# Output stores, two evacuations and the loads of batch 1 in a fused linear-attention and GELU-MLP kernel

## The chip, the core and the metric

The kernel runs on one core of a Trainium2 chip. The metric is the device time of one execution in microseconds (us). Before the change the median of 15 runs is 319.3 us, with runs from 317.35 to 322.01. The engines are called PE (matrix products; PEld is its weight load), DVE (vector), ACT (scalar), POOL (GpSimd) and SP (sync, which here only issues DMAs). An engine's queue is the list of instructions that it executes in order; a DMA is issued by an instruction in one of these queues and then runs by itself.

## The reference

The inputs q, k and v have 8 batches, 8 heads, 576 positions and 64 features, all float32. The attention has no softmax: q and k go through a ReLU, and each is multiplied by a cosine and by a sine of its position.

```
phi(x) = concat(relu(x) * cos(pi/2 * pos/576), relu(x) * sin(pi/2 * pos/576))
kv  = sum over positions of phi(k)^T v          # 128 x 64 per head
z   = sum over positions of phi(k)
x   = (phi(q) kv) / (phi(q) . z + 1e-6)         # 4608 tokens x 512
h   = x w_in                                    # 512 -> 2048
out = (h * sigmoid(1.702 h)) w_out              # 2048 -> 512
```

## The kernel before

**Attention, by batch.** For a batch, three float32 tiles qf, vf and kf are loaded. A main load (load_part, L79) brings positions 0 to 511 and a tail load (load_tail, L84) positions 512 to 575; a main is 1024 KB in rows of 1 KB, a tail 128 KB in rows of 256 bytes. These tiles have two buffers each. Then follow prep_q (L219: ReLU of q into qn, bf16), the transposition of qn (on PE for batches 0 and 1, L234; by DMA on SP for the others, L246), the product with cos and sin (qT, L244 or L256, on DVE), prep_v (L265: v times cos and times sin into vt), prep_k (L258: ReLU of k into kr), unit_kv (L280: 40 small matmuls, then casts zbuf and kvs on DVE), unit_den (L305: 32 matmuls, then the reciprocal on DVE), unit_spread (L330: matmuls, then four copies invb on ACT) and unit_num (L346: 16 matmuls, then four DVE multiplications at L359 by the inverse, "the division", which write xT). unit_spread and unit_num run for two halves of the positions.

**MLP, by block.** The 4608 tokens are cut into 9 blocks of 512 tokens. A block runs 16 tiles of mm1 (L373: four matmuls into a PSUM tile hps, GELU on ACT into g) and then mm2 for four chunks t of 128 tokens (L395: 16 matmuls into a PSUM tile, in four parts of four). After a chunk's last part, the PSUM tile is copied into an SBUF tile ysb (the evacuation, L404 to L408), and one or two DMAs (pieces, L379) store it on SP's queue (L410). ysb comes from ypool with three buffers (L162). hps and yps have two PSUM buffers each. In block 0 the four chunks are computed in turn, part by part (t = n % 4), with chunks 0 and 1 in hps and 2 and 3 in yps; chunks 1 and 3 are copied by DVE (L406), all others by ACT (L408). In the later blocks one chunk follows the other, and ACT copies all. The last chunk of the last block is mm2_last (L412), with its stores on SP and ACT.

**Order.** The order on every engine is the order in which the program emits the instructions. The loop of L483 lays it out by hand in steps n = 0 to 31 of one block: step n emits a tile of mm1 (n < 16) or a part of mm2, and then the attention pieces of the next batch that are listed in work[n]. Steps n = 32 to 39 (L531) hold only such pieces. In block 0, for batch 1, prep_q is at n = 6, prep_v from 8 to 12, prep_k at 13 and 14, unit_kv at 15, unit_den at 18, unit_spread at 22 and 28, unit_num at 25 and 31. So in block 0 the second unit_num stands behind the last part of mm2 and its evacuation, and block 1 begins with mm1, which reads xT of batch 1. In later blocks everything of the next batch starts at n = 0, and the second unit_num is at n = 28, with three parts of mm2 behind it.

**Loads.** Batch 0 is loaded by SP, its tails by ACT. POOL then issues the four pieces of w_in (L454), after a small copy of one element of vf that makes it wait for that load (L452). SP waits for w_in's second piece (L455, a DMA of one element) and issues the mains of batch 1 in the order q, v, k (L457). POOL waits for w_in's third piece (L458), issues the three tails of batch 1 (L459), waits for batch 1's vf (L460) and issues the four pieces of w_out (L462). SP waits for w_out's third piece (L463) and loads batch 2. From batch 3 on, load_all(b + 1) stands behind the DMA transposes of batch b on SP.

Of the kernel before, what the change touches and what calls it, by code (L numbers as in the profile page):

```python
# [12 lines left out]
F32 = mybir.dt.float32  # L13
# [15 lines left out]
def kernel(  # L29
# [9 lines left out]
    nc = tc.nc  # L39
    B, H, S, D = q.shape  # L40
    d_model = H * D
# [21 lines left out]
    def hps_tile():  # L63
        return ps.tile([128, TB], F32, name="hps", bufs=2)

    def yps_tile():
        return ps.tile([128, TB], F32, name="yps", bufs=2)
# [9 lines left out]
    state = {b: {} for b in range(B)}  # L77

    def load_part(t, src, b, h0, h1):  # L79
        nc.sync.dma_start(  # L80
            out=t[:, 256 * h0:256 * h1].rearrange("p (h e) -> p h e", h=h1 - h0),
            in_=src[b, h0:h1, 0:512, :].rearrange("h (p c) d -> p h (c d)", c=4))

    def load_tail(t, src, b, on):  # L84
        on.dma_start(
            out=t[0:64, 2048:2560].rearrange("p (h d) -> p h d", h=H),
            in_=src[b, :, 512:576, :].rearrange("h p d -> p h d"))

    SRC = (("qf", q), ("vf", v), ("kf", k))

    def load_new(b):
        for name, _ in SRC:
            state[b][name] = two.tile([128, 2560], F32, name=name)

    def load_tails(b, on):
        for name, src in SRC:
            load_tail(state[b][name], src, b, on)

    def load_mains(b):
        for name, src in SRC:  # L100
            load_part(state[b][name], src, b, 0, H)
# [57 lines left out]
    tmp.close()  # L159

    gpool = ctx.enter_context(tc.tile_pool(name="gpool", bufs=18))
    ypool = ctx.enter_context(tc.tile_pool(name="ypool", bufs=3))  # L162

    kr = one.tile([128, 5, NP, 128], BF16, name="kr")
    vt = one.tile([128, 5, H, VW], BF16, name="vt")
# [35 lines left out]
    w_in_sb = one.tile([128, NP, d_ff], BF16)  # L201
# [171 lines left out]
    def mm1(i, fc):  # L373
        hps = hps_tile()
        for kc in range(NP):
            mm1_part(hps, i, fc, kc)
        gelu(hps, fc)

    def pieces(m):  # L379

        got, g = [], m * 128
        while g < m * 128 + 128:
            b, r = divmod(g, S)
            if r < 512:
                n = min(128 - r % 128, m * 128 + 128 - g)
                got.append((g - m * 128, n, b * S + 4 * (r % 128) + r // 128, 4))
            else:
                n = min(S - r, m * 128 + 128 - g)
                got.append((g - m * 128, n, b * S + r, 1))
            g += n  # L390
        return got

    cur = {}

    def mm2(i, t, part):  # L395

        if part == 0:
            cur[t] = hps_tile() if i == 0 and t < 2 else yps_tile()
        yps = cur[t]
        for fc in range(part * 4, part * 4 + 4):  # L400
            nc.tensor.matmul(yps, gT[fc][:, ds(t * 128, 128)], w_out_sb[:, fc, :],  # L401
                             start=(fc == 0), stop=(fc == FC - 1))
        if part == 3:
            ysb = ypool.tile([128, d_model], F32, name="ysb")  # L404
            if i == 0 and t % 2:
                nc.vector.tensor_copy(ysb, yps)  # L406
            else:
                nc.scalar.copy(ysb, yps)  # L408
            for (p0, n, row, step) in pieces(i * 4 + t):
                nc.sync.dma_start(out=out[row:row + (n - 1) * step + 1:step, :], in_=ysb[p0:p0 + n, :])  # L410

    def mm2_last(i, t):  # L412

        yps = yps_tile()
        ysb = ypool.tile([128, d_model], F32, name="ysb")
        hd = d_model // 2
        for n in range(2):
            cols = ds(n * hd, hd)
            if n == 1:
                yps = yps_tile()  # L420
            for fc in range(FC):
                nc.tensor.matmul(yps[:, 0:hd], gT[fc][:, ds(t * 128, 128)], w_out_sb[:, fc, cols],  # L422
                                 start=(fc == 0), stop=(fc == FC - 1))
            if n == 0:
                nc.scalar.copy(ysb[:, cols], yps[:, 0:hd])
            else:
                nc.vector.tensor_copy(ysb[:, cols], yps[:, 0:hd])  # L427
            for m, (p0, cnt, row, step) in enumerate(pieces(i * 4 + t)):
                (nc.sync if m == 0 else nc.scalar).dma_start(out=out[row:row + (cnt - 1) * step + 1:step, cols],
                                                             in_=ysb[p0:p0 + cnt, cols])  # L430


    junk = const.tile([1, 16], F32)
# [20 lines left out]
        nc.gpsimd.dma_start(out=w_in_sb[:, :, ts(g, 512)], in_=win_r[:, :, ts(g, 512)])  # L454
    nc.sync.dma_start(out=junk[:, 8:9], in_=w_in_sb[0:1, 0, 1022:1024].bitcast(F32))  # L455
    load_new(1)
    load_mains(1)  # L457
    nc.gpsimd.tensor_copy(junk[:, 2:3], w_in_sb[0:1, 0, 1534:1535])  # L458
    load_tails(1, nc.gpsimd)  # L459
    nc.gpsimd.tensor_copy(junk[:, 1:2], state[1]["vf"][0:1, 0:1])  # L460
    for g in range(4):
        nc.gpsimd.dma_start(out=w_out_sb[:, ts(g, 4), :], in_=wout_r[:, ts(g, 4), :])  # L462
# [20 lines left out]
    for i in range(NBLK):  # L483
        work = {n: [] for n in range(40)}
        b = i + 1

        def at(n, f, *a):
            work[n].append(lambda: f(*a))

        if b < B:  # L490
            k0 = 6 if i == 0 else 0
            at(k0, prep_new, b)
            at(k0, prep_q, b, 0)
            at(k0, prep_q, b, 1)
            if i == 0:
                for j in range(NP):
                    at(k0 + 2 + j, transpose_pe, b, j, 0)
                    at(k0 + 2 + j, transpose_pe, b, j, 1)
            else:
                at(k0, transpose_dma, b)  # L500
                if b + 1 < B:
                    at(k0 + 1, load_all, b + 1)
            for c in range(5):
                for cs in range(2):
                    at(k0 + 2 + c, prep_v, b, c, cs)
            at(k0 + 7, prep_k, b, 0, 4)
            at(k0 + 7, prep_k_tail, b)
            at(k0 + 8, prep_k, b, 4, 8)
            if i > 0:
                for j in range(NP):  # L510
                    at(k0 + 9 + j, prep_trig, b, j)
            k1 = 15 if i == 0 else 12
            at(k1, unit_kv, b)
            at(k1 + 3, unit_den, b)
            for hf in range(2):
                at(k1 + 7 + 6 * hf, unit_spread, b, hf)
                at(k1 + 10 + 6 * hf, unit_num, b, hf)
        for n in range(32):
            if n < FC:
                if i > 0 or n > 3:  # L520
                    mm1(i, n)
            elif i == 0:
                mm2(i, n % 4, (n - FC) // 4)
            elif i == NBLK - 1 and n >= 28:
                if n == 28:
                    mm2_last(i, 3)
            else:
                mm2(i, (n - FC) // 4, n % 4)
            for f in work[n]:
                f()  # L530
        for n in range(32, 40):  # L531
            for f in work[n]:
                f()


# [28 lines left out]
```

## Time and profile before

| what | us |
|---|---|
| median of 15 runs | 319.3 |
| the profiled execution: its time | 319.18 |
| its span, first to last instruction | 317.2 |
| PE busy | 301.1 |
| DVE busy | 135.4 |
| ACT busy | 135.5 |
| POOL busy | 18.6 |
| first mm1 of block 1 starts | 64.19 |
| first mm1 of block 2 starts | 98.36 |
| last evacuation (DVE, L427) ends | 313.49 |

All numbers of the prediction come from one profiled execution. A line of a timeline gives start, duration, engine, line, operation, tiles written and read, and in brackets how long the engine had been idle and what ended that. Several equal instructions in a row are one line with xN, whose duration is that of the whole group. Instructions that overlap in a pipeline have durations longer than the distance between their starts. In a table of stages, the number behind the busy times is the clock that PE was granted (1.00 is full speed), then the share of time in which the DMA engines were busy, and GB/s. "To landing" is the time from a DMA's issue to its completion. A DMA with a cast (w_in and w_out) is counted by the bytes that it writes, half of those that it reads.

### The profile page before, as it was taken

How to read it: one execution, taken by the hardware profiler on the slowest of the kernel's cores; microseconds unless marked ns; L12 is line 12 of the kernel's file. 1: busy time of each engine (PE TensorE's matmuls, PEld its weight loads, DVE VectorE, ACT ScalarE, POOL GpSimd, SP SyncE). 2: the span in 40 equal slices, each digit the busy share in tenths (PEclk: the TensorE clock that was granted, in tenths of full speed). 3: DMA queues.
4: the chain of work that ended last, by engine and by line, in shares of the span. 5: the costliest groups of instructions: out<-in, count | busy, mean ns of one | idle time of the engine just before them, and what ended most of it. 6: DMA issues, size and time to landing. Idle time of an engine off the chain costs nothing.

```text
span 317.2 us, 5510 instructions
## 1 busy us (share of the span) xinstructions
PE 301.1 (95%) x2178; PEld 140.4 (44%) x2216; DVE 135.4 (43%) x344; ACT 135.5 (43%) x260; POOL 18.6 (6%) x56
## 2 busy tenths in 40 slices
PE   8799979689999999999999999999999999999994
PEld 3344544234444544454445444444444444444443
DVE  4852864195319451954193618541854110000000
ACT  5544511336334634363436343634462446217511
POOL 7802400000000000000000000000000000000000
PEclk9999999979999999999999999999999999999999
DMA  7999999936923495349435953593330220011022
GB/s 209 267 205 293 243 187 294 274 74 199 286 67 85 108 354 111 100 132 331 96 83 141 336 97 98 158 320 82 83 60 0 69 66 0 35 66 33 2 66 66
DMA packets 60908, 45.83 MB, mean 144 GB/s; under 512 B 27380, under 2 KB 56308, under 8 KB 60884
## 3 DMA queue, kind: packets, MB, share of 16 engines
q1 hardware_dynamic: 54772, 40.38, 47.6%
q0 software_dynamic: 4368, 4.59, 8.9%
q10 hardware_dynamic: 1744, 0.52, 0.8%
q8 instruction: 17, 0.28, 0.4%
q14 instruction: 7, 0.06, 0.1%
HBM read 36.70 MB, written 9.44 MB: 145 GB/s over the span
## 4 chain that ended last, share of the span: by engine, by line
PE 82%; DMA 11%; DVE 3%; issue 1%; SPq 1%; POOL 0%; ACT 0%; DVEq 0%; ACTq 0%
PE yps L401 36%; PE hps L365 36%; DMA vf<-in_v_dram 7%; PE at L288 3%; PE at L356 3%; DMA w_in_sb<-in_moe_w_in_dram 2%; PE hps L401 2%; DMA out_dram<-ysb 2%; DVE vt L277 1%; PE at L314 1%; PE yps L422 1%; PE at L338 1%; DVE qT L244 1%; DVE kr L217 0%; POOL w_in_sb L454 0%
## 5 line engine op out<-in xcount | busy, mean ns | idle before, releaser
L365 PE MATMUL hps<-xT,w_in_sb 128*128 128x512 bf16 x551 | 127.6, 382 | 5.0 <-DVE xT L359 3.8
L401 PE MATMUL yps<-w_out_sb,g 128*128 128x512 bf16 x509 | 118.8, 380 | 0.9 <-issue 0.2
L370 ACT ACTIVATE g<-hps 128x512 bf16<-128x512 f32 x142 | 84.7, 597 | 58.3 <-PE hps L365 55.6
L365 PEld LDWEIGHTS <-w_in_sb 128*128 128x128 bf16 x576 | 55.7, 98 | 72.6 <-issue 9.0
L401 PEld LDWEIGHTS <-g 128*128 128x128 bf16 x560 | 51.9, 98 | 63.4 <-issue 2.9
L408 ACT COPY ysb<-yps 128x512 f32<-128x512 f32 x32 | 18.7, 585 | 83.4 <-PE yps L401 54.1
L359 DVE TENSOR_TENSOR xT<-at,invb 128x288 bf16<-128x288 f32 x64 | 24.7, 450 | 62.0 <-PE at L356 62.0
L343 ACT COPY invb<-at 128x288 f32<-128x288 f32 x60 | 19.7, 419 | 21.0 <-PE at L338 21.0
L256 DVE TENSOR_TENSOR qT<-qTr,trig 128x1152 bf16<-128x1152 bf16 x24 | 16.6, 754 | 22.4 <-DMA qTr<-qn 19.8
L427 DVE COPY ysb<-yps 128x256 f32<-128x256 f32 x1 | 0.4, 425 | 56.7 <-PE yps L422 56.7
L277 DVE TENSOR_SCALAR vt<-vf,cosw 128x512 bf16<-128x512 f32 (+1 forms) x40 | 19.2, 488 | 1.2 <-DMA vf<-in_v_dram 1.2
L217 DVE TENSOR_SCALAR qn<-qf 128x512 bf16<-128x512 f32 (+2 forms) x52 | 14.2, 342 | 8.5 <-DMA qf<-in_q_dram 8.5
L277 DVE TENSOR_SCALAR vt<-vf,sinw 128x512 bf16<-128x512 f32 (+1 forms) x36 | 17.6, 490 | 0.0
L75 PE MATMUL hps<-warm 128*128 128x512 bf16 x47 | 13.8, 455 | 1.2 <-DVE halfpi L121 1.2
L288 PE MATMUL at<-vt,kr 128*64 128x130 bf16 x320 | 10.9, 221 | 3.6 <-ACT kr L215 1.8
L356 PE MATMUL at<-qT,kvs 64*64 64x288 bf16 x256 | 12.2, 289 | 0.4 <-ACT invb L343 0.3
L288 PEld LDWEIGHTS <-kr 128*64 128x64 bf16 x320 | 9.3, 109 | 7.2 <-issue 2.5
L217 DVE TENSOR_SCALAR kr<-kf 128x1024 bf16<-128x1024 f32 (+1 forms) x23 | 12.3, 588 | 0.0
L356 PEld LDWEIGHTS <-kvs 64*64 64x64 bf16 x256 | 6.4, 105 | 8.0 <-issue 7.7
L75 PEld LDWEIGHTS <-warm 128*128 128x128 bf16 x47 | 5.0, 113 | 8.3 <-issue 3.9
L401 PE MATMUL hps<-w_out_sb,g 128*128 128x512 bf16 x30 | 7.6, 380 | 0.1
L323 DVE RECIPROCAL den<-den 128x144 f32<-128x144 f32 x7 | 7.4, 1053 | 0.2
(79 smaller groups left out, 98.3 us busy)
## 6 DMA issues: line engine op xcount, KB each, us to landing
qf<-in_q_dram SPq DMA_DIRECT2D x8, 1024.0 KB, 6.6
vf<-in_v_dram SPq DMA_DIRECT2D x8, 1024.0 KB, 9.4
kf<-in_k_dram SPq DMA_DIRECT2D x7, 1024.0 KB, 12.2
out_dram<-ysb SPq DMA_DIRECT2D x38, 128.0 KB, 2.4
out_dram<-ysb SPq DMA_DIRECT2D x16, 256.0 KB, 2.3
w_in_sb<-in_moe_w_in_dram POOLq DMA_DIRECT2D x4, 512.0 KB, 8.9
w_out_sb<-in_moe_w_out_dram POOLq DMA_DIRECT2D x4, 512.0 KB, 9.4
kf<-in_k_dram SPq DMA_DIRECT2D x2, 512.0 KB, 11.4
```

The lines of the kernel that those rows point to most:

```text
L75: nc.tensor.matmul(wps, warm[:, 0:128], warm, start=True, stop=True)
L217: on.tensor_scalar(o, i, 0.0, None, op0=MAX)
L256: nc.vector.tensor_tensor(s["qT"][:, j], s["qTr"][:, j].unsqueeze(1).to_broadcast([128, 2, S]), trig, op=MUL)
L277: on.tensor_scalar(o, i, w, None, op0=MUL)
L288: nc.tensor.matmul(kv4[j // 2][w:w + 64, j % 2], kr[:, c, j, 64 * hh:64 * hh + 64], vt[:, c, 2 * j + hh, :], start=(c == 0), stop=(c == 4))
L343: nc.scalar.copy(invb, bps[j][:, 0:HF])
L356: nc.tensor.matmul(num_ps[j][w:w + 64, 0:HF], s["kvs"][j][r:r + 64, cs, :], s["qT"][r:r + 64, j, cs, ds(hf * HF, HF)], start=(cs == 0), st ...
L359: nc.vector.tensor_tensor(xT[:, j, ds(b * S + hf * HF, HF)], t[:, 0:HF], s["invb"][j, hf], op=MUL)
L365: nc.tensor.matmul(hps, w_in_sb[:, kc, ds(fc * 128, 128)], xT[:, kc, ds(i * TB, TB)], start=(kc == 0), stop=(kc == NP - 1))
L370: nc.scalar.activation(g, hps, AF.Gelu_apprx_sigmoid)
L401: nc.tensor.matmul(yps, gT[fc][:, ds(t * 128, 128)], w_out_sb[:, fc, :], start=(fc == 0), stop=(fc == FC - 1))
L408: nc.scalar.copy(ysb, yps)
```

## The change

Four things are edited. ypool gets a fourth buffer. The evacuation becomes a function of its own, evac, whose stores are issued by POOL instead of SP; the stores of mm2_last stay where they were. In block 0 the chunks t = 0 and 1 are evacuated by ACT after their last part, and chunks 2 and 3 by DVE after the whole of block 0's work, that is behind the second unit_num of batch 1 and its division. The six loads of batch 1 are all issued by SP, in the order main of q, tail of q, main of v, tail of v, tail of k, main of k; POOL's wait for w_in's third piece goes.

```diff
-    ypool = ctx.enter_context(tc.tile_pool(name="ypool", bufs=3))
+    ypool = ctx.enter_context(tc.tile_pool(name="ypool", bufs=4))
...
-        if part == 3:
-            ysb = ypool.tile([128, d_model], F32, name="ysb")
-            if i == 0 and t % 2:
-                nc.vector.tensor_copy(ysb, yps)
-            else:
-                nc.scalar.copy(ysb, yps)
-            for (p0, n, row, step) in pieces(i * 4 + t):
-                nc.sync.dma_start(out=out[row:row + (n - 1) * step + 1:step, :], in_=ysb[p0:p0 + n, :])
+        if part == 3 and (i > 0 or t < 2):
+            evac(i, t)
+
+    def evac(i, t, on=None):
+        ysb = ypool.tile([128, d_model], F32, name="ysb")
+        if on is nc.vector:
+            nc.vector.tensor_copy(ysb, cur[t])
+        else:
+            nc.scalar.copy(ysb, cur[t])
+        for (p0, n, row, step) in pieces(i * 4 + t):
+            nc.gpsimd.dma_start(out=out[row:row + (n - 1) * step + 1:step, :], in_=ysb[p0:p0 + n, :])
...
-    load_mains(1)
-    nc.gpsimd.tensor_copy(junk[:, 2:3], w_in_sb[0:1, 0, 1534:1535])
-    load_tails(1, nc.gpsimd)
+    for name, src in SRC:
+        if name == "kf":
+            load_tail(state[1][name], src, 1, nc.sync)
+        load_part(state[1][name], src, 1, 0, H)
+        if name != "kf":
+            load_tail(state[1][name], src, 1, nc.sync)
     nc.gpsimd.tensor_copy(junk[:, 1:2], state[1]["vf"][0:1, 0:1])
...
         for n in range(32, 40):
             for f in work[n]:
                 f()
+        if i == 0:
+            for t in range(2, 4):
+                evac(i, t, nc.vector)
```

## The prediction

> **What bounds the kernel now.** I read the page first: engine shares, then the 40 slices, then the chain of work that ended last.
>
> ```profile
> span 317.2 us, 5510 instructions
> ...
> PE 301.1 (95%) x2178; PEld 140.4 (44%) x2216; DVE 135.4 (43%) x344; ACT 135.5 (43%) x260; POOL 18.6 (6%) x56
> ...
> PE   8799979689999999999999999999999999999994
> ```
>
> PE is busy 95% of the span, and after slice 8 (about 65 us) it is never below nine tenths until the end. So nothing on DVE, ACT, POOL or SP earns time in the later blocks unless it makes PE wait there. What can be won lies where PE has holes: before 65 us. The list of waits names two that the change touches. The larger is in the chain between 56 and 68 us (start, length, what):
>
> ```profile
> 57.84 5.12 DMA out_dram<-ysb
> ...
> 63.08 0.06 DVE ysb L406
> ...
> 63.69 0.46 DVE xT L359
> ...
> 64.19 2.96 PE hps L365 x7
> ```
>
> The DVE timeline says why:
>
> ```profile
> 58.13 0.69 DVE L406 COPY ysb<-hps 128x512 f32<-128x512 f32 x1 [2.53 <-PE hps L401]
> 63.08 0.69 DVE L406 COPY ysb<-yps 128x512 f32<-128x512 f32 x1 [4.26 <-DMA out_dram<-ysb]
> 63.69 1.54 DVE L359 TENSOR_TENSOR xT<-at,invb 128x288 bf16<-128x288 f32 x4
> ```
>
> The fourth evacuation of block 0 needs a fourth ysb; three exist, so DVE waits until the first store has landed (62.96). Behind it in DVE's order stand the four divisions (L359) that block 1's first matmuls read. PE ended unit_num of batch 1 at 60.43 and starts mm1 of block 1 at 64.19. The wait has an after-effect. Stages of 1 us, PE alone (busy, instructions, granted clock, DMA share, GB/s):
>
> ```profile
> 64.00:65.00 1.00, 0.81 (x3) 1.00 0.37 141
> 65.00:66.00 1.00, 1.00 (x3) 0.61 0.33 121
> 66.00:67.00 1.00, 1.00 (x3) 0.50 0.00 0
> 67.00:68.00 1.00, 0.78 (x3) 0.50 0.00 0
> 68.00:69.00 1.00, 1.00 (x4) 0.68 0.66 131
> 69.00:70.00 1.00, 1.00 (x7) 1.00 0.52 108
> ```
>
> After a hole of 3.76 us the granted clock falls to half for about 3.4 us. The second hole is in block 0:
>
> ```profile
> 35.01 0.49 DVE L277 TENSOR_SCALAR vt<-vf,cosw 128x512 bf16<-128x512 f32 x1 [1.23 <-DMA vf<-in_v_dram]
> ...
> 42.08 1.70 PE L288 MATMUL at<-vt,kr 128*64 128x130 bf16 x40 [1.63 <-DVE kr L217]
> ```
>
> DVE works without a gap from 35.01, when batch 1's vf lands, to the end of kr at 42.97; unit_kv waits for it and takes 1.70 us with a stop inside (its next runs take 1.32). So about 2.0 us of PE time hang on DVE's start, hence on vf's landing.
>
> **Part 1: evacuations of t=2 and t=3 behind the division, four buffers.** Either edit alone removes the wait on the store. DVE is then free from 55.6 on, since t=1 goes to ACT. ACT copies t=0 at 56.92, the four invb at 57.40 to 58.71, then t=1 until about 59.3, where it now copies t=2. Nothing of ACT's is due before the first gelu, and mm1 needs t=1's hps buffer only at its second tile. In blocks 1 and 2 the first division starts 0.54 us after unit_num's first matmul (88.90 to 89.44, 95.14 to 95.69). unit_num starts at 59.75, so the division starts at 60.29, lasts 0.45, and mm1 starts 0.05 later, at 60.79. Saved: 64.19 - 60.79 = **3.40 us**. What is late next is the division itself: kc=1 to 3 come at DVE's pace (0.36 us each, as before at 64.19, 64.55, 64.92, 65.28), which is in both kernels.
>
> The hole left is 0.36 us. The 1.63 us hole at 40.45 left the granted clock at 1.00 in every stage behind it, so I take the half-clock stretch as gone. Before, the starts from 65.28 to 68.65 are 8 intervals in 3.37 us; later blocks run 45 matmuls in 9.71 us, 0.216 each, so 8 take 1.73. Saved: **1.65 us** (0 if the clock falls all the same).
>
> The two copies come back on DVE behind the division: 2 x 0.61 us (start to start). DVE's preparation of batch 2 starts at 61.74 + 1.22 = 62.96, 2.17 us after mm1's start instead of 0.95, and mm1 itself now runs 1.65 us faster. The cover: unit_kv(2) falls at 77.80 - 3.40 - 1.65 = 72.75, kr is ready 7.4 us after 62.96, at 70.4. The thin place is unit_den(2): 81.79 - 5.05 = 76.74. It needs qT and zbuf. SP's transposes start 1.78 us after prep_q's start (66.92 against 65.14): 64.74; first qT 8.21 us later (75.13 against 66.92): 72.95; four qT 2.68 and four zbuf casts 0.74: 76.37. Slack 0.37 us, where it was 2.26. In blocks 2 and 3 the same stretch from transposes to qT took 8.77 and 8.66 us, 0.5 longer, and prep_q may be stretched (part 2). I charge **0.2 us**, bounds 0 and 0.9.
>
> **Part 2: stores on POOL's queue.** 52 issues leave SP (0.48 us median) for POOL, which is idle after 38.3. The nearest rows are POOL's own issues: 0.70 us (tails at 24.1), 0.77 (w_out), 0.92 to 1.46 (w_in), so at most 76 us on an idle engine. For SP this frees its order: in block 2 SP held the transposes until 100.42 behind the last store, while qn was ready at about 99.0. PE does not wait for those transposes (zbuf ends at 112.60, unit_den runs at 113.62), so I price the gain at 0; it only widens that slack by 1.4 us. A store that lands later is harmless: ysb is written again four chunks of 2.9 us or more later. The price could be on DVE: while POOL issued w_out, the 128x512 vt copies with sinw averaged 605 ns against 478 later, +0.13 us per instruction met. The place that counts is the division at a block's end (95.69 to 97.24, next mm1 at 98.36: cover 1.12 us). But the eight divisions at 22.14 to 25.15 ran at 447 to 457 ns each, also beside POOL's tail issues. So 0, bounds 0 and 0.5. At the end, the last POOL store is issued about 310.3 to 311.9 (old time). w_out's first piece landed 6.0 us after issue with 2.6 us of transfer at 200 GB/s; a quarter of the bytes makes about 4, so 315.1, against 315.7 for the final stores on SP and ACT: 0, bounds 0 and 1.5.
>
> [...]
>
> **Part 3: batch 1's tails on SP between the mains.** Today POOL waits for w_in (24.01), then issues three tails that share the DMA engines with the mains; between 28.8 and 32.2 the rate drops from about 370 to 215 GB/s. qf lands at 31.21, vf at 34.98, 3.77 later. Now only one tail stands ahead of vf on SP, and kf's tail goes ahead of kf's main. Two prices. By bytes, two tails (0.26 MB at 190 GB/s) leave vf's way: 1.4 us. By batch 2's mains, back to back on SP, which landed at 54.5, 57.6 and 61.1, vf comes 3.1 us behind qf plus one tail of 0.4 to 0.7 (batch 2's three took about 2 us of transfer): 3.5 to 3.8, a gain of 0 to 0.3. Gain is also capped at 1.5, since DVE's chain has PE's transpose at 32.40 before it. Against: qf's own tail, needed at 31.8, may come later by a few tenths. I take **0.6 us**, bounds -0.3 and 1.5. kf's main landed at 38.2 and is needed at 41.34, so its moving back and an earlier w_out beside it are covered by 3 us. w_out itself is first read at 43.70, some 2.5 us after its first piece landed.
>
> **Sum**, against the profiled execution's own 319.18 us (span 317.2 and 2.0 around it; the runs' median is 319.3): 319.18 - 3.40 - 1.65 - 0.6 + 0.2 = **313.7 us**.
>
> **Rivals.** (a) The loads gain all they can, 1.5 us, and block 1 hides everything: 319.18 - 5.05 - 1.5 = 312.6. For it: the rate dip. Against: the spacing of batch 2's mains. 0.13. (b) The late transposes take the stall's place: unit_den waits 0.9 and the loads give nothing: 315.0. For it: the slack of 0.37. 0.14. (c) The clock falls to half even so, since PE is only half loaded while it follows the division: 313.7 + 1.65 = 315.4. 0.05. (d) The change doesn't remove the stall, because something else holds DVE or the first division; only the loads move: about 318.6, the same within 0.3% (about 1 us, roughly what a measurement of this kernel can tell from no change). No row speaks for it: DVE is idle from 55.6. 0.05. (e) Slower: POOL's issues hold DVE out at each block's last division. If the two store issues of t=2 take 1.46 us each, as w_in's longest, and DVE stands still meanwhile, xT is 2.92 - 1.12 = 1.8 us late in 6 blocks: 313.7 + 10.8 = 324.5. It decides from 2.2 us of hold per block ((5.45 + 1) / 6 + 1.12). Against it: divisions unchanged beside POOL's tails. 0.05. The forecast has 0.58. Faster 0.58 + 0.13 + 0.14 + 0.05 = 0.90, same 0.05, slower 0.05.
>
> **Range.** Low: (a) with run spread, 312.3. High: the forecast with the upper costs of parts 1 and 2 and no gain from part 3 (0.9, 0.5, 0.6) reaches 315.5; with (c) partly in, 316.0. Left out: (d), (e) and tails, some 0.15 to 0.2.
>
> **What would show it.** Right: no wait of DVE on the store; mm1 of block 1 starts about 0.4 us after unit_num's end; clock 1.00 through the following 5 us; the hole before unit_kv(1) at 1.0 to 1.6 us; SP's transposes right behind prep_q. Wrong: a PE wait for qT or zbuf at unit_den(2); a wait for xT at later block starts; DVE rows lengthened beside POOL's issues; vf landing no earlier; or an end in which POOL's store is last.

## The result and the profile after

The median is 315.27 us (9 runs, 314.97 to 316.31) against 319.13 us for the kernel before (47 runs): a ratio of 0.9882, 95% interval 0.9861 to 0.9903. That is 3.9 us less, where 5.5 had been forecast; the time lies within the stated range. The ratios, here and below, leave out executions more than 1.5% slower than the fastest of the same kernel (two of e6, one of e8, one of the kernel before beside e5 to e8). The profiled execution took 315.16 us, 4.02 less than that of before. The page of the changed kernel:

```profile
span 313.2 us, 5606 instructions
...
PE 300.2 (96%) x2178; PEld 139.2 (44%) x2216; DVE 135.5 (43%) x344; ACT 135.4 (43%) x260; POOL 47.1 (15%) x106
...
PE   8799989999999999999999999999999999999994
```

The slice with a 6 has gone, and PE is at nine tenths to the end. The chain around the start of block 1 (start, length, what) holds no DMA any more:

```profile
58.86 0.42 PE at L356 x8
...
59.34 0.47 DVE xT L359
59.81 0.04 issue
59.85 2.12 PE hps L365 x7
```

On DVE the division now comes first, and the two copies behind it:

```profile
59.34 1.55 DVE L359 TENSOR_TENSOR xT<-at,invb 128x288 bf16<-128x288 f32 x4 [4.69 <-PE at L356]
60.81 1.28 DVE L409 COPY ysb<-yps 128x512 f32<-128x512 f32 x2
62.00 1.89 DVE L217 TENSOR_SCALAR qn<-qf 128x512 bf16<-128x512 f32 x7
```

PE's stages of 1 us behind it (busy, instructions, granted clock, DMA share, GB/s) keep the full clock:

```profile
60.00:61.00 1.00, 1.00 (x4) 1.00 1.39 194
61.00:62.00 1.00, 0.97 (x4) 1.00 1.02 342
62.00:63.00 1.00, 0.98 (x5) 1.00 0.33 123
```

In block 0, vf lands 0.93 us earlier, and unit_kv follows it by as much:

```profile
34.08 0.49 DVE L277 TENSOR_SCALAR vt<-vf,cosw 128x512 bf16<-128x512 f32 x1 [0.86 <-DMA vf<-in_v_dram]
```

```profile
41.12 1.70 PE L288 MATMUL at<-vt,kr 128*64 128x130 bf16 x40 [1.17 <-DVE kr L217]
```

So far all is as forecast or better. The surprise is behind it. Places of the two traces, in us:

| place on PE | before | after | gained so far |
|---|---|---|---|
| unit_kv(1) starts | 42.08 | 41.12 | 0.96 |
| block 1, first mm1 | 64.19 | 59.85 | 4.34 |
| unit_kv(2) starts | 77.80 | 71.81 | 5.99 |
| block 2, first mm1 | 98.36 | 92.37 | 5.99 |
| block 3 | 130.19 | 124.45 | 5.74 |
| block 5 | 193.86 | 188.61 | 5.25 |
| block 8 | 285.15 | 280.65 | 4.50 |
| last copy ends | 313.49 | 309.24 | 4.25 |

At block 2 the kernel is 5.99 us ahead. Then it gives back 0.25 us in each of the blocks 2 to 8, 1.74 in all, though no engine shows a wait. The GELUs show where. Some in a row on ACT, three before and four after (block 4; start, duration, idle before):

```profile
163.09 0.60 ACT L370 ACTIVATE g<-hps 128x512 bf16<-128x512 f32 x1 [0.23 <-PE hps L365]
163.95 0.60 ACT L370 ACTIVATE g<-hps 128x512 bf16<-128x512 f32 x1 [0.27 <-PE hps L365]
164.81 0.60 ACT L370 ACTIVATE g<-hps 128x512 bf16<-128x512 f32 x1 [0.27 <-PE hps L365]
```

```profile
162.01 0.60 ACT L370 ACTIVATE g<-hps 128x512 bf16<-128x512 f32 x1 [0.27 <-PE hps L365]
162.92 0.60 ACT L370 ACTIVATE g<-hps 128x512 bf16<-128x512 f32 x1 [0.31 <-PE hps L365]
163.78 0.60 ACT L370 ACTIVATE g<-hps 128x512 bf16<-128x512 f32 x1 [0.27 <-PE hps L365]
164.69 0.60 ACT L370 ACTIVATE g<-hps 128x512 bf16<-128x512 f32 x1 [0.31 <-PE hps L365]
```

Before, they come every 0.86 us; after, every second one is 0.04 later, and two tiles of mm1 take 1.77 us instead of 1.73. The traces say what differs, since they list the semaphores that each instruction waits for. ACT's part of one later block (whose work each waits for in brackets; DMA waits, and the copies invb, left out):

```
before:  ysb<-yps copy x4   [PE, ACT]
         g<-hps GELU  x16   [PE]
after:   ysb<-yps copy x4   [PE, ACT]
         g<-hps GELU  x2    [PE]
         g<-hps GELU  x14   [PE, ACT]
```

This fits the author's reading of where this program has its waits, which is **theory M**: an ACT instruction that overwrites a buffer has a wait for the one that wrote it last, on ACT itself too, unless an earlier wait of ACT has covered that point. g has 18 buffers, so from its third tile on a block overwrites tiles of the block before. With three ysb buffers, t=3's buffer was last written in the same block, behind all its GELUs: its copy's wait on ACT covers them all, and the next block's GELUs need none. With four, the copy's wait goes back to the block before, so 14 GELUs of every block carry a second wait. (Which instruction a wait aims at is worked out from the order of the buffers; the trace names only the semaphore.) In the trace such a GELU has a semaphore instruction of its own ahead of it: the kernel before has 15 of them, 14 in block 1 and one in block 0, the changed one 113, 14 in each of blocks 1 to 8. hps has two buffers, so the GELU of tile n lies on the path to tile n + 2.

### The profile page after: what moved, and what is told of

It reads as the page before. It is cut to its first block, busy times and chain, and to the rows that moved or that the text cites. A ratio compares the mean times of both kernels' runs of the same rounds, so it can differ in the third digit from the quotient of the medians.

```text
span 313.2 us, 5606 instructions
## 1 busy us (share of the span) xinstructions
PE 300.2 (96%) x2178; PEld 139.2 (44%) x2216; DVE 135.5 (43%) x344; ACT 135.4 (43%) x260; POOL 47.1 (15%) x106
## 4 chain that ended last, share of the span: by engine, by line
PE 84%; DMA 6%; DVE 3%; POOL 2%; issue 1%; ACT 1%; ACTq 1%; SPq 1%; DVEq 0%; POOLq 0%
PE yps L401 37%; PE hps L365 36%; DMA vf<-in_v_dram 4%; PE at L356 3%; PE at L288 3%; DMA w_in_sb<-in_moe_w_in_dram 3%; PE hps L401 2%; DVE vt L277 1%; PE at L314 1%; PE yps L425 1%; PE at L338 1%; ACTq L85 1%; DVE qT L244 1%; POOL by_row L187 1%; DVE kr L217 0%
## 5 line engine op out<-in xcount | busy, mean ns | idle before, releaser
L365 PEld LDWEIGHTS <-w_in_sb 128*128 128x128 bf16 x576 | 54.9, 97 | 70.2 <-issue 10.1
L413 POOL DMA_DIRECT2D out_dram<-ysb x54 | 30.6, 569 | 239.4 <-ACT invb L343 129.7
L75 PE MATMUL hps<-warm 128*128 128x512 bf16 x47 | 12.5, 419 | 1.2 <-DVE halfpi L121 1.2
```

Source lines behind the costliest of these rows:

```text
L75: nc.tensor.matmul(wps, warm[:, 0:128], warm, start=True, stop=True)
L365: nc.tensor.matmul(hps, w_in_sb[:, kc, ds(fc * 128, 128)], xT[:, kc, ds(i * TB, TB)], start=(kc == 0), stop=(kc == NP - 1))
L413: nc.gpsimd.dma_start(out=out[row:row + (n - 1) * step + 1:step, :], in_=ysb[p0:p0 + n, :])
```

## The experiments

Rivals: **P**, the stores on POOL disturb PE; **S**, tiles moved in SBUF change the pace; and later **L**, below. Times are medians; "held" is the number of executions whose granted clock was 0.996 or more over the span (one stretch of 3.4 us at half clock takes it to 0.995, two to 0.989; half clock behind the last matmul, which costs nothing, lowers it too: e1's profile shows 0.991 with one stretch ahead of it). The runs came in three series, each beside its own executions of the kernel before, with medians of 319.70 (e1 to e4), 319.27 (e5 to e8) and 318.90 us (e9 to e12); across series the ratios compare better than the times.

| run | us (lowest to highest) | ratio to before, 95% | held | block 3 to 4, us |
|---|---|---|---|---|
| changed kernel | 315.27 (314.97 to 316.31) | 0.9882 (0.9861 to 0.9903) | 8 of 9 | 32.08 |
| e1_three_bufs | 315.31 (313.90 to 317.74) | 0.9859 (0.9806 to 0.9912) | 2 of 6 | 31.83 |
| e2_act_read | 314.16 (313.60 to 317.24) | 0.9844 (0.9790 to 0.9899) | 3 of 6 | 31.83 |
| e3_sp_stores | 315.57 (314.76 to 318.44) | 0.9880 (0.9829 to 0.9931) | 4 of 6 | 32.08 |
| e4_old_loads | 318.42 (316.18 to 319.84) | 0.9944 (0.9912 to 0.9977) | 3 of 12 | 32.08 |
| e5_move_only | 316.32 (314.12 to 318.68) | 0.9903 (0.9866 to 0.9939) | 2 of 11 | 31.83 |
| e6_four_only | 316.73 (315.59 to 321.41) | 0.9918 (0.9883 to 0.9952) | 5 of 12 | 32.08 |
| e7_pool_only | 319.73 (318.45 to 321.51) | 1.0013 (0.9985 to 1.0041) | 0 of 12 | 31.83 |
| e8_loads_only | 320.33 (317.89 to 323.15) | 1.0010 (0.9978 to 1.0043) | 0 of 12 | 31.83 |
| e9_three_read | 314.67 (313.87 to 317.61) | 0.9879 (0.9835 to 0.9922) | 3 of 6 | 31.83 |
| e10_filler | 316.07 (314.02 to 316.92) | 0.9896 (0.9857 to 0.9936) | 6 of 6 | 31.83 |
| e11_kv_later | 315.20 (313.37 to 317.76) | 0.9881 (0.9836 to 0.9926) | 5 of 6 | 31.83 |
| e12_old_loads_filler | 316.46 (316.30 to 317.62) | 0.9932 (0.9904 to 0.9961) | 10 of 10 | 32.08 |

**e1_three_bufs** and **e2_act_read** test M from two sides, against the changed kernel.

```diff
# e1
-    ypool = ctx.enter_context(tc.tile_pool(name="ypool", bufs=4))
+    ypool = ctx.enter_context(tc.tile_pool(name="ypool", bufs=3))
# e2, ypool with 4, in the loop over n, behind the step's mm1 or mm2
+            if n == FC:
+                nc.scalar.copy(junk[:, 3:4], gT[FC - 1][0:1, 0:1])
```

> The changed kernel with ypool back at three buffers, nothing else. Theory M (the fourth buffer costs the gain): with four buffers no evacuation makes ACT wait for its own work of the same block, so 14 GELUs in each of blocks 1 to 8 carry a wait of their own on ACT besides the one on PE; each starts 0.06 us later and PE loses about 0.25 us per block. With three buffers this is left in block 1 alone: 7 x 0.25 = 1.75 us less, 315.3 - 1.75 = 313.5 us, block 2 starts 31.8 us before block 3 instead of 32.1. No wait on a store comes back, because t=3's copy now stands behind the division. Rival P (the 54 store issues on POOL slow the matmuls): unchanged, 315.3. Rival S (the tiles' places in SBUF): no number of its own; it expects a change of the pace in every block, block 1 too.

> The changed kernel with its four buffers, plus one ACT copy of a single element of the block's last g at the first step of mm2 in every block. It makes ACT wait once per block for its own work, at a place where ACT is idle. Theory M: the second wait goes from all GELUs, in block 1 too: 8 x 0.25 = 2.0 us less, 313.3 us, though four buffers and the stores on POOL stay. Rival P: unchanged, 315.3. Rival S: unchanged, 315.3, since no tile of any pool moves.

Both bring the block back to 31.83 us. e2 does it with four buffers and with the stores on POOL, and moves no tile: P and S fall, M stands. In block 1 e2 shows only 0.04 of M's 0.25 us (32.48 instead of 32.52): mm1 is faster there, but unit_den(2) then takes 0.2 us longer. In e2's trace one semaphore instruction is left ahead of a GELU, and block 4's GELUs are even again:

```profile
161.72 0.60 ACT L370 ACTIVATE g<-hps 128x512 bf16<-128x512 f32 x1 [0.27 <-PE hps L365]
162.59 0.60 ACT L370 ACTIVATE g<-hps 128x512 bf16<-128x512 f32 x1 [0.27 <-PE hps L365]
163.45 0.60 ACT L370 ACTIVATE g<-hps 128x512 bf16<-128x512 f32 x1 [0.27 <-PE hps L365]
```

In time, e2's three held executions took 313.60 to 313.94 and e1's two 313.90 and 314.04, against 314.97 to 315.92 in the changed kernel's eight. Neither median reached M's 313.5 and 313.3 us, and they are nearer to 315.27 because more executions of e1 and e2 lost the clock. e1's profile shows such a one, in block 0:

```profile
43.35 1.95 PE L288 MATMUL at<-vt,kr 128*64 128x130 bf16 x32 [3.14 <-DVE kr L217]
```

```profile
42.00:43.00 1.00, 0.00 (x0) 0.90 1.14 165
43.00:44.00 1.00, 0.65 (x13) 0.50 1.10 172
44.00:45.00 1.00, 1.00 (x24) 0.50 1.24 205
```

vf had landed at 36.30 here, 2.2 us later than in the changed kernel's profile with the same loads, and the hole of 3.14 us before unit_kv(1) cost half the clock for 3.4 us.

**e3_sp_stores**: evac issues on SP (nc.gpsimd becomes nc.sync).

> The changed kernel with evac's stores on SP again; four buffers, moved evacuations and new loads stay. Theory M: mm1's pace stays slow and the stores are worth nothing to PE, 315.3 within 0.3. Rival P: 313.5. If freeing SP's order was worth something (transposes earlier): over 315.6, with a PE wait at unit_den.

The pace is the changed kernel's and so is the time; P falls again. One small cost of POOL's stores remains: from the last matmul's start to the end of the span it is 4.65 to 4.96 us in the nine profiles with mm2's stores on POOL and 4.34 to 4.53 in the five with them on SP, about 0.3 us. What takes it there was not tried.

**e4_old_loads**: the changed kernel with the three old lines for the loads of batch 1.

> The changed kernel with the loads of batch 1 as before: mains on SP, tails on POOL. If the 0.92 us by which vf landed earlier comes from the new order of the loads: 315.3 + 0.9 = 316.2, the hole before unit_kv(1) back at about 1.6 us. If it is the scatter of one execution's landings: 315.3 within 0.3.

2.2 us slower than the higher of the two expectations. In its profile the hole is 2.41 us and the clock falls, as in 9 of 12 executions; the changed kernel lost it in 1 of 9.

```profile
43.83 1.36 PE L288 MATMUL at<-vt,kr 128*64 128x130 bf16 x28 [2.41 <-DVE kr L217]
```

```profile
44.00:45.00 1.00, 0.93 (x28) 1.00 1.24 205
45.00:46.00 1.00, 1.00 (x21) 0.53 1.22 203
```

From this came theory **L**: the loads count less by the time at which they land than by whether the hole before unit_kv(1) gets long enough to cost the clock. Half of it is already in doubt here: e4's three held executions took 316.18 to 317.61 us, the changed kernel's eight 314.97 to 315.92, so about 1 us is left that is not the clock.

**e5 to e8** are each one part alone, on the kernel before.

```diff
# e5: the evacuations' new order; 3 buffers, stores on SP, old loads
# e6
-    ypool = ... bufs=3
+    ypool = ... bufs=4
# e7, in mm2
-                nc.sync.dma_start(out=out[...], in_=ysb[p0:p0 + n, :])
+                nc.gpsimd.dma_start(out=out[...], in_=ysb[p0:p0 + n, :])
# e8: the changed kernel's loop over SRC in place of the old lines
```

> The kernel before with only the order of the evacuations changed (t=1 on ACT, t=2 and 3 on DVE behind the division): three buffers, stores on SP, old loads. All theories expect the wait on the store and the half clock behind it to go. Theory M: no second wait on the GELUs from block 2 on, so a block takes 31.83 us. With vf landing at 35.0 as in the profile of before: 319.3 - 5.05 = 314.3 us. Theory L (the old loads often land later than that profile shows, and the hole before unit_kv(1) then costs the clock too, as in the run of the changed kernel with old loads, 318.4): 318.4 - 1.75 = 316.7 us, with a granted clock under 0.996 in most executions.

> The kernel before with four ypool buffers, nothing else. The wait on the store goes (t=3's copy on DVE then ends about 60.5, just ahead of the division). Theory M: a block takes 32.08 us instead of 31.83 in blocks 2 to 8; 319.3 - 4.9 + 1.75 = 316.2 us. Rival P or a cost of the moved evacuations: the pace stays at 31.83 and the time is 314.4. Theory L adds up to 2 us to either, but not to the pace.

> The kernel before with the stores of mm2 on POOL, nothing else. If the store of t=0 landed late (5.1 us) because it stood behind batch 2's loads in SP's order and queue, it now lands about 2.6 us after its issue at 57.6, the copy of t=3 starts at 60.2 instead of 63.1, and the clock holds: 319.3 - 2.9 - 1.65 = 314.8 us. If its packets wait for the loads on the DMA engines whatever the queue: 318 to 319.3. Pace of the blocks 31.83 by theory M (three buffers), 32.08 by rival P.

> The kernel before with the new loads of batch 1, nothing else. The stall on the store stays. If the new order lands vf 0.9 us earlier and that is all: 319.3 - 0.9 = 318.4 us. By theory L (it also saves the clock from falling at unit_kv(1) in many executions): 317.5 or less, and fewer executions with a granted clock of 0.989 than in the kernel before.

e5 and e6: either edit alone takes away the stall at block 1's start, and only e6 has the slow pace, so M holds on the kernel before as well. Where the clock held, e5 took 314.12 and 314.99 and e6 315.59 to 316.15 (expected 314.3 and 316.2); the medians are higher by the clock, as L said.

e7 gains nothing. The store of t=0 still took 4.79 us, on another queue, among batch 2's loads:

```profile
57.32 4.79 DMA out_dram<-ysb
...
62.84 0.46 DVE xT L359
...
63.34 2.49 PE hps L365 x7
```

e8 gains nothing either, and both expectations failed: 318.4, and L's 317.5 with fewer executions at 0.989 (8 of 12 are at or below it, 17 of 34 of before). unit_kv(1) does start earlier, at 41.37, but the stall behind it is still there, the store lands after 5.66 us, and behind the hole of 4.28 us between matmul starts the half clock lasts twice as long:

```profile
62.00:63.00 1.00, 0.00 (x0) 0.76 0.59 211
...
67.00:68.00 1.00, 0.91 (x3) 0.50 0.22 44
68.00:69.00 1.00, 1.00 (x4) 0.50 0.44 87
69.00:70.00 1.00, 1.00 (x6) 0.82 2.05 139
```

Of the 0.71 us gained at unit_kv(1) in this trace, 0.47 are left at block 1's start, and the longer half clock takes them: unit_kv(2) starts at 77.97, against 77.80 before. Part of that may be luck, by the estimate in the last section.

**e9 to e12** ask whether L is right, and look for the fastest version.

```diff
# e9: e1 and e2 together
# e10: e9, and in the loop's list for block 0; e12: e4 with the same
+            if i == 0:
+                at(k1, warmup, 6)
             at(k1, unit_kv, b)
# e11: e9 with
-            k1 = 15 if i == 0 else 12
+            k1 = 16 if i == 0 else 12
```

> The changed kernel with three ypool buffers and the one-element ACT read per block: the second wait is gone from every GELU, block 1 included. Theory M: 313.3 us where the clock holds, as with four buffers and the read; every block 31.83. Rival to M (the number of buffers itself has a price or a worth): a pace or a time other than that of the four-buffer kernel with the read.

> As e9_three_read, plus 6 matmuls of zeros (no result is used) on PE between the last mm1 tile of block 0 and unit_kv of batch 1. Theory L (what scatters is the half clock: the hole before unit_kv(1) held the clock in the six profiles where it was 1.0 to 2.0 us between matmul starts and lost it in the four where it was 2.8 to 3.7): the hole is cut below 2.8, no execution falls to a granted clock under 0.995, and the median is 313.5 with a narrow spread. If the scatter comes from the landings alone: the spread stays at 3 us or more, and the median goes up by 0.2 to 0.4.

> As e9_three_read, with the second half of batch 1's attention one step later in block 0 (k1 = 16), so that a part of mm2 (4 matmuls, 0.86 us) runs ahead of unit_kv. Theory L: the hole shrinks by 0.86 us by real work; fewer executions lose the clock, best ones gain up to 0.8: 312.6 to 313.3. Against it: the second unit_num then comes behind the last part of mm2 with two parts instead of three after its unit_spread, and PE may wait about 0.3 us there.

> The changed kernel with the loads of batch 1 as before (as e4_old_loads, 318.4 us) and the 6 matmuls of zeros ahead of unit_kv(1). If the 3.1 us between old and new loads are mostly the clock: 316.2 to 316.6, granted clock over 0.996 in most executions. If they are vf's landing itself: 318 to 318.6.

e12 came out where L put it. With six useless matmuls the kernel with the old loads kept the clock in all 10 executions, where e4 lost it in 9 of 12, and 8 of the 10 lie between 316.30 and 316.97. Its median is 2.0 us below e4's (318.42 to 316.46). How much of that is the filler is not settled: the two ran in different series, and by the ratios, whose intervals overlap, it is 0.4 us. The hole is nearly closed:

```profile
42.20 1.70 PE L288 MATMUL at<-vt,kr 128*64 128x130 bf16 x40 [0.23 <-DVE kr L217]
```

```profile
43.00:44.00 1.00, 0.93 (x25) 1.00 1.26 209
44.00:45.00 1.00, 0.95 (x5) 1.00 1.22 203
```

e10 kept the clock in all six executions, as L says, but its spread stayed at 2.9 us and its median is 316.07 instead of 313.5, above e9's, in the same series. So L is shown for the clock, not for the time: the landings themselves count too. e9's rival showed itself as well: with three buffers a second stall appears in block 1 that e2 does not have. On DVE and on PE, in e9:

```profile
60.95 0.68 DVE L409 COPY ysb<-yps 128x512 f32<-128x512 f32 x1
63.35 0.69 DVE L409 COPY ysb<-yps 128x512 f32<-128x512 f32 x1 [1.72 <-DMA out_dram<-ysb]
```

```profile
76.64 1.07 PE L314 MATMUL at<-qT,zbuf 128*32 128x144 bf16 x32 [0.86 <-DVE zbuf L294]
```

With three buffers the wait on the store has not gone; it only stands behind the division, and holds up prep_q of batch 2, its transposes, qT, zbuf, and at last unit_den(2). In e10 the DVE wait was 1.8 us and PE's 1.0; in e1 and e5, also with three buffers, DVE waited 0.2 and 0.7 us and PE's unit_den(2) did not. That accounts for e9's span against e2's (0.9 us more), but for only 1.0 of e10's 2.5; another 1.3 are a later unit_kv(1). What spreads e10's six executions is not settled, as only one was traced. e11 puts real work into the hole, but finds w_out not yet there:

```profile
41.22 1.04 PE L401 MATMUL hps<-w_out_sb,g 128*128 128x512 bf16 x4 [1.09 <-DMA w_out_sb<-in_moe_w_out_dram]
```

The fastest median is e2's, 314.16 us, four buffers with the one-element read. Its interval overlaps that of the changed kernel; the 31.83 against 32.08 us per block does not depend on the scatter.

## Why the prediction was right, and where it was not

The time is within the range, but partly by luck. The range's upper end was made of costs at unit_den(2), on DVE and of loads that gain nothing, and none of these came; a cost that was priced at nothing filled their place. Rival (c) names a time close to the result, 315.4, but its condition did not occur: the clock held.

- **Removal of the stall, 3.40 us**: 3.38 in the trace (4.34 - 0.96). The division started 0.55 us after unit_num's first matmul, 0.54 had been taken from the later blocks.
- **The clock, 1.65 us**: from block 1's first mm1 to unit_kv(2) it took 13.61 us before and 11.96 after, exactly 1.65 less. 17 of the 34 runs of before beside e5 to e8 were at 0.989 or below, so they had two such stretches, both from this stall (as in e8) or one from the hole in block 0; only one execution of before was traced, so which of the two stays open.
- **"Either edit alone removes the wait"** is true for the start of block 1 (e5, e6), but the two are not equal. The step that failed is here: the fourth buffer was priced at nothing. It costs a second wait on 14 GELUs per block, 0.25 us in each of seven blocks that had been free of it, 1.74 us. No row of before shows it except block 1's own GELUs, which had the uneven spacing already; that was overlooked. The cause is shown by e2, which takes the second waits away and keeps the buffers, and by e6, which adds the buffer alone. And the fourth buffer has a use that was not seen either: without it the wait stays behind the division (e9).
- **unit_den(2), charged 0.2 us**: unit_kv(2) to unit_den(2) takes 4.00 us after and 3.99 before, so 0. The thin place was rightly named: 1.7 us more on DVE are a PE hole of 0.9 in e9.
- **Loads, 0.6 us**: 0.96 in the pair of profiles, but 0.6 on average. From qf's issue to vf's first use on DVE, the six profiles with old loads have 13.45 to 14.13 us (mean 13.78) and the eight with new loads 12.61 to 14.12 (13.19). The clock adds about as much, and was left out of the sum: with the stall gone, old loads kept it in 10 of 35 executions (e4, e5, e6) and new ones in 20 of 33 (changed kernel, e1, e2, e3, e9), and a difference of 0.32 at 1.65 us each makes an estimated 0.5 us.
- **Stores on POOL, 0**: right for PE's pace (e3, e7), and about 0.3 us at the end, within the bound of 1.5. POOL took over 54 issues, not 52. In the changed kernel the 54 issues took 569 ns on average, and the longest, 1487 ns, stood beside prep_q of batch 2 on DVE. In e9 one took 4894 ns: it started at 158.66, while DVE worked without a gap, and ended at 163.55, 0.1 us behind the end of DVE's last instruction of that stretch. The first line is POOL's 54 issues in e9 (shortest, median, longest in ns), the second that last instruction:

```profile
L413 POOL DMA_DIRECT2D out_dram<-ysb x54: 527/530/4894, 57.0 to 306.1; - x54
```

```profile
161.83 1.61 DVE L217 TENSOR_SCALAR kr<-kf 128x1024 bf16<-128x1024 f32 x3
```

e9's blocks still took 31.83 us each, as nothing waited for that store. Whether DVE's work made that issue long was not tried. Rival (e) had DVE waiting for POOL; DVE's vt instructions beside that issue ran at 473 ns, as elsewhere.

Sum by the trace: 0.96 + 3.38 + 1.65 - 1.74 = 4.25 to the last copy, less 0.23 at the end, 4.02.

## What to carry to other kernels

A buffer more is not free: by theory M, the number of buffers decides which of the program's waits are already covered. Here the fourth ysb buffer came with one more semaphore wait on 14 GELUs of a block, each on a two-buffer cycle, and block 3 to 4 took 32.08 us instead of 31.83 (e6 against e5). Compare the pace of the loops behind the edit, and the waits that each instruction carries, not only the place that was edited. And price a PE hole with the clock that it may cost, here 1.65 us behind block 1's start: filler matmuls kept the clock in all 16 executions that had them, though whether they pay in time was not settled (e12 against e4, e10 against e9).

## What the runs showed of the hardware that was not expected

- The half clock came behind shorter holes than the 3.76 us of before. With 0.63 to 1.63 us of PE idle before unit_kv(1) the clock held (changed kernel, before, e2, e3, e7, e8, e9); with 2.41, 2.57, 3.14 and 3.28 us (e4, e5, e1, e6) it fell to 0.50 for about 3.4 us.
- A hole's length is not the whole of it. From its first record of 1.00 on, the granted clock stayed at 1.00 for 58.03 us, at 0.50 for 3.41 and at 1.00 for 249.17 in the trace of before, and at 1.00 for 307.20 in that of the changed kernel: about 17, 1, 73 and 90 times 3.41. In the 3.41 us ahead of a fall PE had been idle for 2.4 us (before), and by the stages of 1 us for about 2.6 (e1), 2.2 (e4), 2.4 (e5), 1.9 (e6) and 2.8 (e8). In e4 the clock fell only at 45.06, 1.2 us after the hole's end. In e8 PE was idle for another 1.20 us behind the fall, and the half clock lasted 6.83 us. That first record starts at 7.20 us in the trace of before and at 4.50 in that of the changed kernel. That it is partly luck whether a hole of 2 to 3 us costs the clock is the author's estimate from these times; what decides it was not shown.
- The time at which the same loads land scatters by over 1 us from execution to execution: SP's one-element DMA behind w_in's second piece started at 20.66 us in the trace of the changed kernel, 20.69 in that of before, 21.40 in e1 and 21.91 in e4, ahead of anything that the edits touch. The clock adds to it; that it alone makes the 3 to 5 us of scatter of most of these kernels is not shown, as e10 kept the clock and still scattered by 2.9.
- A semaphore instruction ahead of a GELU stands 0.06 us ahead of it on ACT (14 of the 15 in the trace of before, 112 of the 113 in that of the changed kernel), and two tiles of mm1 then take 1.77 instead of 1.73 us on PE.
